# Retention attention and a gated feed-forward layer on one core: matmul groups and loads placed by the table that already places ScalarE's and VectorE's work

## The chip, the cores and the metric

One core of one Trainium2 chip. The metric is the device time of one execution in microseconds; the kernel before takes 275.86 us (median of 3 runs, 275.59 to 278.33).

## The reference

q, k and v are float32 of shape (8 batches, 8 heads, 576 positions, 64). The first half is attention without a softmax, with a decay per head; the second is a feed-forward layer of 512 to 2048 to 512 on the 4608 rows that the first half gives:

```python
scores = scale * np.matmul(q, k.transpose(0, 1, 3, 2))
gamma = 1.0 - 2.0 ** (-5.0 - np.arange(H))
Dmat = np.where(rel >= 0, gamma[:, None, None] ** rel[None], 0.0)   # rel = row - column
attn = np.matmul(scores * Dmat[None], v)
x = attn.transpose(0, 2, 1, 3).reshape(4608, 512)
h = x @ w_in
g = h * (1.0 / (1.0 + np.exp(-1.702 * h)))
out = g @ w_out
```

## The kernel before, in words

**Units and chunks.** The 4608 rows are 36 units of 128 rows; four units make a chunk of 512 rows, so there are nine chunks, 0 to 8. A unit is loaded in three parts: k and q (`load_kq`, line 358, q of units 1 and 2 by line 345) and v (`load_v`, line 371), all by DMAs that GpSimd issues. Unit 0's k and q come by SyncE (`load_kq0`, line 378).

**Attention of a unit.** k and q are transposed, by TensorE for units 0 to 7 (`transpose_pe`, lines 497 and 502, copied out by line 515 on ScalarE or 518 on VectorE) and by DMA for the others (`dma_transpose`, line 532, issued by SyncE). v is scaled by powers of the decay (`scale_v`). Then follow 64x64 matmuls: `scores` (line 638), masked out of PSUM by VectorE (`scores_out`, line 647); the state, k transposed times v (`state_half`, lines 544 and 554, in the first units; `state_both` and `state_sum` with a cast on ScalarE later); `values` (line 660) and `inter` (line 622), which make x; and `x_out` (line 675) or `x_out_pair` (line 685), which multiplies by a factor table `gq` and writes the transposed x, `xT`. The tables `vfac`, `gq` and `gpow` are made at the start with exponentials on ScalarE (lines 439, 447, 453); `gq_next` (line 470) makes the later parts of `gq` on VectorE from `gpow`.

**Feed-forward of a chunk.** In chunks 0 and 1 the product x times w_in is made directly (`up_group`, line 711, and `up`, line 697), and ScalarE applies the gate function straight from PSUM (lines 716 and 702). In chunks 2 to 8 seven products of half size replace eight (class `UpSet`, matmuls at line 954): four sets of 256 features, each with seven steps of four 128x256 matmuls and a pair of PSUM banks of its own, (X, Y), (C, D), (A, B) and (K, E). ScalarE copies some products out (line 965), VectorE adds others (line 969), ScalarE applies the gate function (line 978). The second matrix is used in the same way (class `Pair`, matmuls at line 821): VectorE makes sums of g (line 802), seven products of 16 matmuls follow, called first to seventh, ScalarE copies (line 834), VectorE adds (line 837), and the rows are stored (`store`, line 726).

**What sets the order.** The program is recorded as a list of operations (`Program.op`) with what each reads and writes; waits come out of that in `settle`. Each engine then executes its own list in the order of a key. For TensorE, GpSimd and SyncE the key is the place in the recording. For ScalarE and VectorE it is looked up in `PLACES` by stage ("early", "first", "second", "mid", "last"), which says how far ahead or behind an operation stands; the lead-in is recorded before any stage, and there these two engines too keep the order of the recording. Five chunks, 3 to 7, share the rows of "mid". `PADS` gives numbers of empty instructions (`nop`) that are put before matmuls in certain stretches.

**The lead-in** (`lead_in`). TensorE first runs matmuls on a cleared tile (`warm_quads`, line 1100, and `warm`, line 1093) whose results nobody reads, and some more between the first units. The recording puts all exponentials of ScalarE first and then one gate function on a dummy tile (`gelu_table`, line 1106), so that the load of that function's table stands ahead of the first real one. GpSimd issues the v of unit 0, units 1 and 2, the first two pairs of w_in (`load_win`, line 393: two DMAs a call, 256 columns), unit 3, four more calls of w_in, and so on.

Of the kernel before, what the change touches and what calls it, by code (L numbers as in the profile page):

```python
# [11 lines left out]
B, H, S, DH = 8, 8, 576, 64  # L12
# [18 lines left out]
class Program:  # L31
# [3 lines left out]
    def __init__(self, places, pads=()):  # L35
        self.ops = []
        self.pads, self.gaps, self.spare, self.wide = pads, 0, 0, True
        self.writers, self.readers = {}, {}
        self.places, self.kind, self.turn = places, None, 0
        self.met = {}  # L40
# [22 lines left out]
    def op(self, eng, fn, reads=(), writes=(), dma=None, ndma=1, after_ops=()):  # L63
# [14 lines left out]
        if eng in ("act", "dve"):  # L78
            o.key, o.label = self.place(eng)
# [73 lines left out]
    def emit(self, eng, handle, sems):  # L153
# [16 lines left out]
PLACES = {  # L170
    ("early", "act"): (
# [8 lines left out]
    ),  # L180
    ("early", "dve"): (
# [1204 lines left out]
```

## Time and profile before

| what | value |
|---|---|
| median of 3 runs | 275.86 us |
| the profiled execution's own time | 277.19 us |
| its span, first to last instruction | 275.4 us |
| TensorE busy | 267.3 us (97%), 4402 matmuls |
| VectorE, ScalarE, GpSimd busy | 215.4, 176.1, 136.4 us |
| mean granted TensorE clock | 0.994 |
| first matmul of the feed-forward layer (line 711) | starts at 14.28 us |
| first product with w_out (line 821) | starts at 54.51 us |
| last matmul ends, span ends | 272.66, 275.4 us |

The profiled execution took 277.19 us, 1.79 us more than its span. Lines of a profile name the source line, the engine, the operation and what it writes and reads; times are microseconds unless marked ns. In the timeline a bracket gives the idle time of the engine before an instruction and what ended it.

### The profile page before, as it was taken

How to read it: one execution, taken by the hardware profiler on the slowest of the kernel's cores; microseconds unless marked ns; L12 is line 12 of the kernel's file. 1: busy time of each engine (PE TensorE's matmuls, PEld its weight loads, DVE VectorE, ACT ScalarE, POOL GpSimd, SP SyncE). 2: the span in 40 equal slices, each digit the busy share in tenths (PEclk: the TensorE clock that was granted, in tenths of full speed). 3: DMA queues.
4: the chain of work that ended last, by engine and by line, in shares of the span. 5: the costliest groups of instructions: out<-in, count | busy, mean ns of one | idle time of the engine just before them, and what ended most of it. 6: DMA issues, size and time to landing. Idle time of an engine off the chain costs nothing.

```text
span 275.4 us, 10512 instructions
## 1 busy us (share of the span) xinstructions
PE 267.3 (97%) x4402; PEld 222.6 (81%) x4402; DVE 215.4 (78%) x420; ACT 176.1 (64%) x345; POOL 136.4 (50%) x167
## 2 busy tenths in 40 slices
PE   8789999999999999999999999999999999999996
PEld 6467568888888788878887888788878887888785
DVE  6825457959999889769996999688969996976681
ACT  7536775556937962796279627961796289608942
POOL 9999999400603927943970975096509020000000
PEclk9979999999999999999999999999999999999999
DMA  9999999999993967998998994999299435003004
GB/s 167 172 201 203 221 209 202 224 152 235 187 161 36 240 132 70 197 284 82 171 218 213 95 181 113 231 100 198 89 234 99 60 106 126 6 2 152 0 2 152
DMA packets 118029, 40.79 MB, mean 148 GB/s; under 512 B 104160, under 2 KB 111328, under 8 KB 117984
## 3 DMA queue, kind: packets, MB, share of 16 engines
q0 software_dynamic: 80800, 22.82, 72.2%
q1 hardware_dynamic: 36320, 16.00, 23.8%
q10 hardware_dynamic: 864, 1.31, 1.3%
q8 instruction: 36, 0.59, 0.9%
q14 instruction: 9, 0.07, 0.1%
HBM read 36.70 MB, written 9.44 MB: 168 GB/s over the span
## 4 chain that ended last, share of the span: by engine, by line
PE 85%; ACT 6%; POOL 3%; DMA 2%; DVE 2%; issue 1%; ACTq 0%; POOLq 0%
PE psB L821 20%; PE psA L821 16%; PE psX L954 4%; PE psK L954 4%; PE psA L954 4%; PE psC L954 4%; PE psD L954 3%; PE psY L954 3%; PE psE L954 3%; PE psB L954 3%; PE psB L711 3%; PE psA L711 3%; ACT vp L482 3%; DMA w_in_sb<-in_moe_w_in_dram 2%; PE psY L660 2%; PE psC L821 1%
## 5 line engine op out<-in xcount | busy, mean ns | idle before, releaser
L358 POOL DMA_DIRECT2D kqn<-in_k_dram x39 | 38.5, 1001 | 65.3 <-DMA kqT<-kqn 54.9
L978 ACT ACTIVATE gT<-part 128x512 bf16<-128x512 f32 (+1 forms) x56 | 46.7, 878 | 3.5 <-DVE part L969 3.5
L371 POOL DMA_DIRECT2D vn<-in_v_dram x40 | 40.0, 1018 | 0.1
L358 POOL DMA_DIRECT2D kqn<-in_q_dram x37 | 36.4, 1000 | 0.0
L486 POOL TENSOR_TENSOR vp<-vn,vfac 128x512 bf16<-128x512 f32 x22 | 23.0, 1086 | 21.9 <-PE psD L954 18.0
L965 ACT ACTIVATE part<-psX 128x512 f32<-128x512 f32 x14 | 8.4, 597 | 35.3 <-PE psX L954 35.3
L834 ACT ACTIVATE osb<-psB 128x512 f32<-128x512 f32 (+1 forms) x25 | 14.8, 591 | 23.9 <-PE psB L821 23.9
L821 PE MATMUL psB<-w_out_sb,gT 128*128 128x256 bf16 x224 | 27.0, 273 | 0.0
L821 PEld LDWEIGHTS psB<-w_out_sb,gT 128*128 128x128 bf16 x224 | 21.3, 98 | 4.2 <-DVE part L969 1.8
L591 ACT ACTIVATE kv<-stm 128x1024 bf16<-128x1024 f32 (+1 forms) x16 | 15.6, 976 | 4.8 <-DVE stm L582 4.7
L647 DVE TENSOR_TENSOR pm<-psC,mask 128x512 bf16<-128x512 f32 (+1 forms) x21 | 12.7, 606 | 6.2 <-PE psC L638 5.7
L821 PE MATMUL psB<-wsum,part 128*128 128x256 bf16 x136 | 16.3, 272 | 0.2
L821 PE MATMUL psA<-w_out_sb,gT 128*128 128x256 bf16 x136 | 16.3, 273 | 0.0
L821 PE MATMUL psA<-wsum,part 128*128 128x256 bf16 x136 | 16.3, 273 | 0.0
L685 DVE TENSOR_TENSOR xT<-psY,gq 128x512 bf16<-128x512 f32 x16 | 10.9, 683 | 6.1 <-PE psY L622 6.1
L802 DVE TENSOR_TENSOR part<-gT 128x1024 bf16<-128x1024 bf16 (+1 forms) x18 | 11.9, 667 | 4.3 <-ACT gT L978 2.0
L802 DVE TENSOR_TENSOR part<-part,gT 128x1024 bf16<-128x1024 bf16 (+1 forms) x18 | 12.0, 672 | 3.3 <-ACT gT L978 3.0
L821 PEld LDWEIGHTS psB<-wsum,part 128*128 128x128 bf16 x136 | 12.9, 97 | 2.0 <-DVE part L802 0.4
L821 PEld LDWEIGHTS psA<-wsum,part 128*128 128x128 bf16 x136 | 13.3, 98 | 1.5
L821 PEld LDWEIGHTS psA<-w_out_sb,gT 128*128 128x128 bf16 x136 | 13.2, 98 | 1.6
L821 PE MATMUL psA<-w_out_sb,part 128*128 128x256 bf16 x120 | 14.5, 273 | 0.0
L482 ACT ACTIVATE vp<-vn,vfac 128x64 bf16<-128x64 f32 x48 | 12.3, 337 | 2.2 <-DVE osb L837 2.2
(233 smaller groups left out, 778.1 us busy)
## 6 DMA issues: line engine op xcount, KB each, us to landing
vn<-in_v_dram POOLq DMA_DIRECT2D x32, 256.0 KB, 5.3
out_dram<-osb SPq DMA_DIRECT2D x26, 256.0 KB, 2.8
kqn<-in_k_dram POOLq DMA_DIRECT2D x31, 128.0 KB, 5.2
kqn<-in_q_dram POOLq DMA_DIRECT2D x31, 128.0 KB, 5.3
w_in_sb<-in_moe_w_in_dram POOLq DMA_DIRECT2D x16, 128.0 KB, 5.8
w_out_sb<-in_moe_w_out_dram POOLq DMA_DIRECT2D x4, 512.0 KB, 10.3
out_dram<-osb SPq DMA_DIRECT2D x10, 128.0 KB, 2.4
vn<-in_v_dram POOLq DMA_DIRECT2D x8, 128.0 KB, 4.9
```

The source lines that it names most:

```text
L358: e.dma_start(kqn[sl][p0 : p0 + n, which, :, :], src[b, :, s0 : s0 + n, :].rearrange("h p d -> p h d"),)
L371: e.dma_start(vn[sl][p0 : p0 + n, :, :], v[b, :, s0 : s0 + n, :].rearrange("h p d -> p h d"))
L482: op("act", lambda e, h=h: e.activation(vp[u % NVP][:, h, :], vn[sl][:, h, :], AF.Copy, scale=vfac[:, ty, h : h + 1]), reads=[f"vn{sl}"] + ...
L486: op(eng, lambda e: e.tensor_tensor(vp[u % NVP].ap(), vn[sl].ap(), vfac[:, ty, :, None].to_broadcast([P, H, DH]), ALU.mult), reads=[f"vn{s ...
L591: op("act", lambda e: e.activation(kv[:, i0 % NKV : i0 % NKV + n, :, :], stm[:, i0 % 8 : i0 % 8 + n, :, :], AF.Copy), reads=[f"stm{(i0 + i ...
L647: op("dve", lambda e: e.tensor_tensor(pm[(u0 // 2) % 2][hh][:, c0:c1].rearrange("p (a i) -> p a i", i=64), ps32(SB[hh])[:, c0:c1].rearrang ...
L711: op("pe", lambda e, a=a, f=f, i=i: e.matmul(bank[b][:, n * i : n * i + n], w_in_sb[:, a, P * f : P * f + P], xT[c % 2][:, a, P * lo : P * ...
L802: op("dve", lambda e, d=d, x=x, y=y, alu=alu: e.tensor_tensor(d, x, y, alu), reads=kx + ky, writes=kd)
L821: op("pe", lambda e, x=x, y=y, t=t, s=not more and t == 0 and k == 0, z=k == NF // 2 - 1: e.matmul(bank[b][:, 256 * t : 256 * t + 256], x, ...
L834: op("act", lambda e: e.activation(dst[0], src[0], AF.Copy), reads=src[1], writes=dst[1])
L954: op("pe", lambda e, x=x, y=y, i=i, s=not more and i == 0 and k == 0, z=k == 1: e.matmul(bank[b][:, 256 * i : 256 * i + 256], x, y, start= ...
L978: op("act", lambda e: e.activation(dst, src, AF.Gelu_apprx_sigmoid), reads=reads, writes=[g_key(self.c, f0 + 2 * i + q, j) for i in range( ...
```

## The change

TensorE's groups of matmuls, GpSimd's work, which is nearly all DMA issues, and SyncE's DMA issues get keys from `PLACES` too, and the lead-in becomes two stages of its own, "start" and "lead", so that everything is placed by the table. A group on TensorE is a run of matmuls recorded one after another from the same source line.

```diff
-    def place(self, eng):
-        if self.kind is None:
-            return len(self.ops) / 1e6, None
+    def place(self, eng, fn):
         n = self.met.get(eng, 0)
-        self.met[eng] = n + 1
+        if eng == "pe":
+            n, line, at = self.met.get(eng, (-1, None, None))
+            new = fn.__code__.co_firstlineno
+            n += at != len(self.ops) or (new != line and line not in self.fill)
+            self.met[eng] = n, new, len(self.ops) + 1
+        else:
+            self.met[eng] = n + 1
         row = self.places.get((self.kind, eng))
...
-        if eng in ("act", "dve"):
-            o.key, o.label = self.place(eng)
+        o.key, o.label = self.place(eng, fn)
```

All rows of `PLACES` are new, `PADS` falls from 483 empty instructions to 223, and the recording of the lead-in changes a little: three more filling matmuls (one of 512, one of 128, one of 256 columns), the state of unit 2 before its mask, two `up_group` calls later or earlier.

```diff
 PADS = (
-    0, 0, 0, 48, 0, 0, 63, 0, 0, 111, 0, 0, 75, 0, 0, 72, 0, 0, 114, 0, 0, 0, 0, 0, 0,
+    0, 0, 24, 0, 0, 0, 0, 0, 0, 0, 0, 0, 0, 4, 0, 87, 0, 0, 108, 0, 0, 0, 0, 0, 0,
 )
...
         def lead_in():
+            pr.stage("start")
+            op("dve", lambda e: e.memset(warmt.ap(), 0.0), writes=["warm"])
+            warm_quads(NQUAD)
+            warm(44, "A", 64)
+            pr.stage("lead")
...
-            warm(2)
+            warm(3)
             scores(2)
             scale_v(2)
+            state_half(2, 0)
+            warm(1, "B", 128)
             scores_out(2, 1, 0)
             scores_out(2, 1, 1)
             up_group(0, 0, 2, 0, 2, "A")
-            state_half(2, 0)
-            up_group(0, 2, 2, 0, 2, "B")
             gq_next(2)
             block1(2)
+            up_group(0, 2, 2, 0, 2, "B")
...
+            up_group(0, 0, 4, 2, 3, "A")
             transpose_pe(3, 1, "D")
             transpose_copy(3, 1, "D", "act")
-            up_group(0, 0, 4, 2, 3, "A")
             scale_v(3)
+            warm(2, "E", 256)
             scores(3)
...
-            warm(1, "E", 256)
```

What comes out of the new keys, read from the order of the two built programs (line numbers of the kernel before):

- **GpSimd, lead-in.** Before: v0, unit 1, unit 2, w_in columns 0 to 511 (two calls), unit 3, w_in. After: v0, k1, q1, k2, v1, v2, q2, v3, q3, k3, then w_in columns 256 to 511, columns 0 to 255, 512 to 767, k4, and so on.
- **TensorE, lead-in.** Before, from the scores of unit 2 on: up A (features 0, 1), state 2, up B (2, 3), attention of unit 2, transposes 3, up A (0 to 3 of unit 2's rows), scores 3, state 3, up B (4, 5), attention of unit 3, up A (4, 5), up B (6, 7), up C, up A, up B. After: scores 2, values 1, state 2 (first half), transposes 3, state 2 (second half), up B (2, 3), filling, scores 3, attention of unit 2, state 3, up A (0, 1), up B (4, 5), up A (0 to 3 of unit 2's rows), attention of unit 3, up B (6, 7), up A (4, 5), transposes 4, up B, up C, up A.
- **ScalarE, lead-in.** Before: 8 `vfac`, 4 `gq`, 4 `gpow`, table load, dummy gate function, then copies and gate functions alone; two table loads in all. After: table load, 8 `vfac`, copies, 4 `gq`, copies, `gpow` 1, copies, `gpow` 3, table load, gate function B (2, 3), table load, `gpow` 2, copy of the state of unit 3, table load, gate functions A (0, 1), B (4, 5), A (unit 2's rows), table load, `gpow` 4, table load, gate functions B (6, 7), A, and so on. Six table loads in all. A wait for a matmul stands at the gate function itself, behind the table load. `gelu_table` comes far behind.
- **VectorE, lead-in.** Setting up `iota_k` (line 429), which `vfac` waits for, moves behind the copies of unit 0's transposes.
- **Chunks 3 to 7, TensorE.** Before, the steps of sets X and C go in turn to their end, then those of A and K. After, the first steps of A and K stand between those of X and C, and the last steps of C and X between those of A and K; X's first step stands before the seventh product of the chunk before. The two blocks of attention keep their places, after the second and after the fifth product; inside them the state comes first or last.
- **GpSimd, chunks 3 to 7.** `scale_v` stands among the loads of the next chunk's units instead of behind them, so that the k of one unit and parts of two others are issued behind it. **SyncE**: two of the DMA transposes are issued between the stores of a chunk.

More of the change, by code (lines that the diff above doesn't have):

```diff
@@ L170 @@
 PLACES = {
-    ("early", "act"): (
[8 rows of a table removed]
+    ("start", "dve"): (
+        -9584670,
+    ),
+    ("start", "pe"): (
+        -8800216, -8582703,
+    ),
+    ("lead", "sp"): (
+        -451697, -452173,
+    ),
+    ("lead", "pool"): (
[4 rows of a table added]
+    ),
+    ("lead", "dve"): (
[5 rows of a table added]
+    ),
+    ("lead", "act"): (
[4 rows of a table added]
+    ),
[5 rows of a table added]
+    ),
[5 rows of a table added]
+    ),
+    ("early", "act"): (
[9 rows of a table added]
     ),
     ("early", "dve"): (
[5 rows of a table removed]
[6 rows of a table added]
+    ),
+    ("early", "pool"): (
+        110206, 109859, 107357, 112473, 50897, -39076, 112855, 125682, 42485, 109146, 113018, 81942, 145058,
+        142043, 144901, 137192, 198067, 176992,
+    ),
@@ L187 @@
+    ("early", "sp"): (
+        -514600, -475513, -380993, -322704, -153042, -115303, 69107, -74529,
     ),
     ("first", "dve"): (
[3 rows of a table removed]
[4 rows of a table added]
+    ),
+    ("first", "pe"): (
+        -1937, -911, -20270, -13780, 8996, 9042, -570, 1909, 3048, 2016, 5822, 12976, 42978, 13882, 23184,
+        15326, 15338, 15367, 31518,
     ),
     ("first", "act"): (
-        -116183, -73138, -75013, -72486, -55435, 31948, -42066,
+        -202134, -204784, -158822, -158667, -158598, 19905, -133306,
+    ),
+    ("first", "sp"): (
+        -174005, -88323, -11463, -15312,
+    ),
@@ L216 @@
+    ("mid", "sp"): (
+        12098, 6275, 26602, 28763, 95465, 77092, 30886, 116485,
+    ),
[5 rows of a table added]
     ),
     ("last", "act"): (
[3 rows of a table removed]
[3 rows of a table added]
     ),
     ("last", "dve"): (
[3 rows of a table removed]
[3 rows of a table added]
+    ),
+    ("last", "sp"): (
+        90402, 21097, 55314, 210415,
     ),
@@ L1095, in warm @@
                    reads=["warm"], writes=[b])
+                pr.fill.add(pr.ops[-1].fn.__code__.co_firstlineno)
         def warm_quads(n):
```

27 lines of the change are left out of this document (20 added, 7 removed), and 106 rows, old and new, of the table PLACES.

## The prediction

> **What bounds the kernel now.** I read the page's slices first, then the idle times in TensorE's timeline, then the chain that ended last, then the other engines' timelines where TensorE waits or runs slowly. The slices:
>
> ```profile
> PE   8789999999999999999999999999999999999996
> ...
> PEclk9979999999999999999999999999999999999999
> ```
>
> TensorE is busy from end to end, and only the third slice (14 to 21 us) has a lowered clock. Its timeline, its real work from 14 us on:
>
> ```profile
> 14.28 1.60 PE L711 MATMUL psA<-xT,w_in_sb 128*128 128x256 bf16 x8 [1.62 <-DMA w_in_sb<-in_moe_w_in_dram]
> ...
> 16.17 1.89 PE L711 MATMUL psB<-xT,w_in_sb 128*128 128x256 bf16 x8
> ...
> 19.57 1.07 PE L711 MATMUL psA<-xT,w_in_sb 128*128 128x128 bf16 x16 [0.31 <-DVE xT L675]
> ...
> 25.60 1.04 PE L711 MATMUL psB<-xT,w_in_sb 128*128 128x256 bf16 x8
> 26.48 1.03 PE L697 MATMUL psA<-xT,w_in_sb 128*128 128x512 bf16 x4
> ```
>
> The first product with w_in waits 1.62 us for its DMA, and the first two groups take about twice the 0.87 us that such a group takes later. The windows by half microseconds say why:
>
> ```profile
> 14.50:15.00 0.50, 0.50 (x5) 0.40 (x4) 0.00 (x0) 0.00 (x0) 0.50 (x2) 0.62 2.28 172
> ...
> 17.50:18.00 0.50, 0.50 (x6) 0.09 (x5) 0.00 (x0) 0.00 (x0) 0.50 (x2) 0.50 1.41 189
> 18.00:18.50 0.50, 0.50 (x37) 0.43 (x40) 0.00 (x0) 0.40 (x1) 0.50 (x2) 0.97 1.44 193
> ```
>
> (PEclk is the third number from the right: half from about 14.6 to 18.03.) After 30 us TensorE's bracketed idle times are 0.20, 0.42, 0.27 and 0.32 us, 1.2 in all. From there on the kernel is TensorE's own work: a chunk takes 27.4 us (150.57 to 177.97) whatever else happens. So lost time in the lead-in goes straight to the end, and time can be won only in small joints. The chain at such a joint, the end of an up phase:
>
> ```profile
> 175.19 0.44 PE psA L954 x4
> 175.63 0.46 PE psK L954 x4
> 176.09 0.49 PE psB L954 x4
> 176.57 0.49 PE psE L954 x4
> 177.06 0.44 PE psA L954 x4
> 177.50 0.47 PE psK L954 x4
> ```
>
> **The change, part by part.**
>
> *1. w_in behind unit 3.* The loads on GpSimd:
>
> ```profile
> 7.67 2.47 POOL L393 DMA_DIRECT2D w_in_sb<-in_moe_w_in_dram  x4
> 10.10 0.93 POOL L358 DMA_DIRECT2D kqn<-in_k_dram  x1
> 10.99 0.93 POOL L358 DMA_DIRECT2D kqn<-in_q_dram  x1
> 11.86 0.94 POOL L371 DMA_DIRECT2D vn<-in_v_dram  x1
> 12.74 4.99 POOL L393 DMA_DIRECT2D w_in_sb<-in_moe_w_in_dram  x8
> ```
>
> Unit 3's three issues take 12.74 - 10.10 = 2.64 us and now stand first. The chain has the second half of the first w_in call issued at 8.29 and landed after 5.94 us; so the first w_in (columns 256 to 511, which TensorE uses first) lands at 8.29 + 2.64 + 5.94 = 16.87, and the first up group starts at 16.9: **+2.6 us**. Landings of w_in ran from 4.3 to 6.4 us, so 15.2 to 17.3. An early landing helps little: v3 must land before VectorE can scale it (issued 7.67, v's median 6.4 us, so 14.1), and then VectorE still has this scaling (0.68), a mask (0.41), `gq_next` (0.68), a mask and two `x_out` (0.41 each) before x of unit 1 is complete, about 16.8. That VectorE sets up `iota_k` late, so that `vfac` and the first `scale_v` start 1.5 us later, is swallowed by the same wait.
>
> *2. Work done ahead.* The transposes of unit 3 (8, at 18.64 and 18.88, 0.45 together) and two state halves (0.15 each) move before the first up group, and the 0.31 us idle at 19.57 goes: -1.05.
>
> *3. The clock.* Before, 16 matmuls of 256 columns took 1.61 + 1.82 us between 14.28 and 18.06 instead of 1.75: 1.7 lost. Afterwards TensorE idles at least as long before the first up group, so I let the clock drop again and come back at the same time; only 16.9 to 18.05 then pays half: 0.6, so -1.1. If it needs another stretch of the same length (3.4 us, to 21.45) it is +0.6; if it never drops, -1.7.
>
> *4. ScalarE's tables.* The table load costs:
>
> ```profile
> 5.51 1.28 ACT L1106 ACT_TABLE_LOAD   x1
> 6.80 0.21 ACT L1106 ACTIVATE tblt<-warmt 128x4 bf16<-128x4 bf16 x1
> ```
>
> Before, this switch is hidden. Now exponentials for `gpow` 2 and 4 stand between gate functions: four more loads. First pair: up B ends at 18.35, gate function (0.60) to 19.0, load 20.28, `gpow` 20.4, copy of the state 20.75, load 22.05, gate function A 22.65. TensorE meanwhile has filling 0.2, scores 0.25, attention of unit 2 0.5, state 0.15, up A and up B 0.87 each and 0.3 of joints: at 21.5 it needs bank A again and waits **1.15**. Second pair: up A' to 23.55, its gate function to 24.2, loads and `gpow` 4 to 26.9, gate function B to 27.5; TensorE reaches bank B at 23.55 + 0.7 (attention 3) + 0.87 + 0.44 + 0.45 (transposes 4) + 0.25 = 26.3 and waits **1.2**. Up B, C, A add 2.3: the lead-in's groups end at 29.8, where before they ended at 26.48, or 26.93 with the transposes of unit 4, which now lie before. **Sum of the lead-in +2.9** (2.6 - 1.05 - 1.1 + 2.35 = 2.8, the rest is rounding). Behind it wait ScalarE's copies of unit 4; they are 0.6 us each against 0.87 per up group, so the backlog drains. Bounds: +0.5 if both pairs are covered, +4.1 with the late clock and the latest landing.
>
> The Trainium skill, "ScalarE: Activation LUTs" (What ACT_TABLE_LOAD costs), advises batching calls by table set and puts a switch at 2.66 us, 1.28 for the load and 1.38 for a drain. The row has the 1.28 exactly and no drain: the load starts where the last `gpow` ends (5.03 + 0.48) and the next function at its end.
>
> *5. Chunks 2 to 8.* The order spreads the last groups of the up phase: between two uses of bank A or E stand four or five groups of 0.44 us instead of three, so the 0.46 to 0.49 above should become 0.44. That is 0.17 us an up phase (165.58 to 177.97 is 12.39 against 28 times 0.4365), times 7: **-1.2**. The first product of the chunk takes 1.91 instead of 1.75 and waits for the same addition, three groups back as before: 0. So bounds are 0 and -2.3 (0.33 times 7) for the waits. The extra breaks between 64x64 groups and products in chunk 2 cost 0.1 to 0.15 each: 0.15, within the rounding.
>
> *6. The queues.* GpSimd now has `scale_v` ahead of some loads of the next chunk: the k of such a unit is issued about 3.5 us after the up phase starts, lands 5.2 us later and goes through a 3.0 us transpose by about 14; scores need it after 12.4 + 3.5 us. Two transposes now stand ahead of a store, 5.4 us for four; the row buffers are needed again 12 us later. Both covered by about 2 us or more: 0, and 0.5 us a chunk if the cover fails (+3.5 over seven).
>
> *7. Empty instructions.* Chunk 7's up phase has none, chunk 6's 114; both periods are 27.40 us. 0. The four idles after 30 us (1.2) belong to orders that all change; I count 0, from -1.2 to +1.
>
> The tail (last matmul at 272.66, end at 275.4) keeps its last product, copy and store: 0. **Sum: +2.9 - 1.2 = +1.7.** Against the profiled execution's own 277.19 us that is 278.9; that run was 1.33 above the median, so I forecast 277.6 against 275.86.
>
> **The rivals.**
>
> *A: TensorE never waits after 30 us* (not slower). Place: every joint of chunks 1 to 8; price: the 0.33 us at the end of each up phase and at the first product, seven times, and the four idles, 3.5 us; it decides once more than 2.9 is found. 275.86 + 2.9 - 3.5 = 275.3. For it: the greater distances. Against: the first product keeps its distance.
>
> *B: the reloads hide.* ScalarE waits 3.63 us for psA at 15.92 before, so a load can vanish there; if other work fills TensorE, lead-in +0.5: 275.86 + 0.5 - 1.2 = 275.2. Against it: after each gate function ScalarE has 3.3 us to do and TensorE reuses the bank after about the same.
>
> *C: the new queues starve the steady chunks*, 0.5 us each: 275.86 + 2.9 + 3.5 = 282.3. For it: GpSimd is full for whole 10 us windows there (10.00 at 180 to 190). Against: 2 us of cover.
>
> *D: each table switch also empties the engine*, a load's length again four times: 277.6 + 4 times 1.28 = 282.7. The row at 5.51 speaks against it. By the Trainium skill's page above it would be 4 times 1.38, so 283.1.
>
> *E: nearly all excess in the joints goes* (0.57 us a chunk, from products of 1.85 to 1.91 instead of 1.75 too, 4.0 over seven) and the reloads hide: 275.86 + 0.5 - 4.0 = 272.4. Against: half of it stands where attention meets products, and those places stay.
>
> **How the numbers follow.** Forecast 46%, A 14%, B 14%, C 14%, D 4%, E 8%. 1% is 2.76 us, about what a measurement can tell from no change: below 273.1 faster, above 278.6 slower. Faster: E and 2% of A and B, 0.10. Slower: C, D and the part above 278.6 of the forecast's own range (276.2 to 279.6, three tenths of its 46%), 0.32. Within: 0.58. The range goes from 273.3 to 281.2: it leaves out E's lower side, D and most of C.
>
> **What would show it.** Right: in the changed profile the first line 711 group starts near 16.9, six table loads stand on ScalarE, TensorE idles about 1 us before two line 711 groups at about 22 and 27 us, and the first product with w_out starts about 2.5 to 3 us later than 54.51; later chunks take 27.2. Wrong: the first product at 54.5 or earlier, chunks below 27.0, or waits on DMA in the chunks.

## The result, and the profile after

The changed kernel takes 286.37 us (median of 4 executions, 285.06 to 288.19) against 276.7 us of the kernel before in the same sitting: 1.0349 times as long, 95% interval 1.0266 to 1.0432. That is slower, by 9.7 us; the forecast was 277.6 us and its range ended at 281.2. (Ratios leave out executions that lie over 1.5% above the fastest of their kernel.)

The slices of the page, TensorE's busy tenths and its granted clock, of the changed kernel:

```profile
PE   7796999999899999999999899999998999999995
...
PEclk9897999999999999999999999999999999999999
```

TensorE is still busy from end to end, 267.8 us of a span of 283.2, so busy time hides where 7.8 us went. But the clock is now low in two slices, the second and the fourth, where it was low in one, the third. The span, cut at four places in TensorE's timeline, tells more (starts and ends of the profiled executions, us; `no_reload` and `five` are runs told below):

| stretch | before | changed | no_reload | five |
|---|---|---|---|---|
| to the first group of `up` (line 796 after) | 26.48 | 31.41 | 29.25 | 26.24 |
| from there to the first product with w_out | 27.87 | 27.32 | 26.81 | 26.99 |
| from there to chunk 3's first product with w_out | 68.84 | 69.82 | 68.69 | 69.03 |
| from there to the end of the last matmul | 149.45 | 151.40 | 151.26 | 148.75 |
| tail | 2.76 | 3.25 | 3.19 | 2.98 |
| span | 275.4 | 283.2 | 279.2 | 274.0 |

The two profiled executions took 277.19 and 285.06 us, the one above its kernel's median and the other below, so their difference is 7.9 and not 9.7. Of the 7.8 us between the spans the lead-in has 4.9, the stretch up to chunk 3's first product 1.0, the rest 2.0 and the tail 0.5; the second stretch is 0.55 shorter. (The transposes of unit 4, 0.45 us, have moved from the second stretch to the first. The third stretch does not end at chunk 2's first product, because 32 matmuls of scores and 32 of values stand ahead of that product in the changed order and behind it in the kernel before; cut here, the third and the fourth stretch hold the same matmuls in both kernels. The timeline starts the first product with w_out of the kernel before at 54.35; the chain, from which the prediction's 54.51 came, gives starts some 0.1 to 0.2 later.) The lead-in, TensorE's timeline:

```profile
17.16 1.05 PE L810 MATMUL psB<-xT,w_in_sb 128*128 128x256 bf16 x8
...
20.27 1.03 PE L810 MATMUL psB<-xT,w_in_sb 128*128 128x256 bf16 x8
23.95 1.05 PE L810 MATMUL psA<-xT,w_in_sb 128*128 128x128 bf16 x16 [2.65 <-DVE pm L746]
...
25.68 1.89 PE L810 MATMUL psB<-xT,w_in_sb 128*128 128x256 bf16 x8
...
29.20 1.03 PE L810 MATMUL psB<-xT,w_in_sb 128*128 128x256 bf16 x8
...
31.41 1.03 PE L796 MATMUL psB<-xT,w_in_sb 128*128 128x512 bf16 x4
```

One idle time of 2.65 us stands before the group at 23.95, and the group at 25.68 takes 1.89 us, about twice the 1.05 of the others. GpSimd issues the first w_in at 10.26 us, 2.59 later than before, behind unit 3 as told:

```profile
9.38 0.90 POOL L457 DMA_DIRECT2D kqn<-in_k_dram  x1
10.26 3.73 POOL L492 DMA_DIRECT2D w_in_sb<-in_moe_w_in_dram  x6
```

ScalarE at the time of the idle stretch:

```profile
18.23 1.28 ACT L815 ACT_TABLE_LOAD   x1
19.53 0.60 ACT L815 ACTIVATE winsum<-psB 128x512 bf16<-128x512 f32 x1
20.14 1.28 ACT L552 ACT_TABLE_LOAD   x1
21.44 0.20 ACT L552 ACTIVATE gpow<-lng 128x4 f32<-128x4 f32 x1
21.55 0.36 ACT L653 ACTIVATE kv<-psK 128x256 bf16<-128x256 f32 x1
21.92 1.28 ACT L815 ACT_TABLE_LOAD   x1
...
25.66 1.28 ACT L552 ACT_TABLE_LOAD   x1
26.95 0.20 ACT L552 ACTIVATE gpow<-lng 128x4 f32<-128x4 f32 x1
27.16 1.28 ACT L815 ACT_TABLE_LOAD   x1
28.46 0.60 ACT L815 ACTIVATE winsum<-psB 128x512 bf16<-128x512 f32 x1
```

The loads are there as forecast, 1.28 us each, and each starts within 0.02 us of the end of the function before it. The Trainium skill, "ScalarE: Activation LUTs" (What ACT_TABLE_LOAD costs), has 2.66 us for a switch with its drain; no drain shows here either. The bracket at 23.95 names VectorE's mask, but in the built order the group waits for two other things: `x_out` of unit 2, which ends at 22.81 + 0.41 = 23.22, and the gate function that empties bank A, which ends at 23.21 + 0.60 = 23.81. The group starts 0.14 us after the later one, so ScalarE ends the wait. (`x_out` is late by the same loads: `gpow` 2 at 21.44 releases `gq_next`, and that `x_out`.) And the first load, at 18.23, is not hidden either: it stands behind `gpow` 3 at 18.02, and bank B has been full since 17.16 + 1.05 = 18.21.

The windows of TensorE's clock around the slow group (the third number from the right is the granted clock):

```profile
25.00:26.00 1.00, 1.00 (x43) 0.81 (x43) 0.22 (x1) 0.94 (x2) 1.00 (x3) 0.63 1.82 186
26.00:27.00 1.00, 1.00 (x7) 0.69 (x6) 1.00 (x3) 0.99 (x2) 1.00 (x3) 0.50 1.62 274
27.00:28.00 1.00, 1.00 (x9) 0.88 (x8) 0.13 (x1) 0.99 (x2) 1.00 (x3) 0.50 1.46 212
28.00:29.00 1.00, 1.00 (x12) 0.88 (x10) 0.00 (x0) 0.99 (x3) 1.00 (x3) 0.66 1.94 176
```

0.63 over the first microsecond means half clock from 25.26 on, 0.66 over the last until 28.68: 3.4 us, behind the idle time that began at 21.3. An earlier stretch of the same length (11.6 to 15.0) falls on filling matmuls and attention.

Later the chain that ended last runs through the loads again and again, where before it stays on TensorE: DMA has 13% of the whole chain and TensorE 68%, before 2% and 85%. One such place, in chunk 4, from the chain:

```profile
146.77 0.99 POOL vp L585
147.76 5.47 DMA kqn<-in_k_dram
...
153.24 1.24 SPq L631
...
154.58 6.85 DMA kqT<-kqn
...
161.47 0.21 PE psC L737
```

GpSimd scales a v (0.99) ahead of issuing a k; k lands 5.47 us later, SyncE issues the transpose then, and that takes 6.85 us. TensorE's scores at 161.47 wait 0.88 us for it:

```profile
161.47 0.21 PE L737 MATMUL psC<-kqT 64*64 64x64 bf16 x1 [0.88 <-DMA kqT<-kqn]
```

The times between the starts of the chunks' products (chunks 3 to 7) are 28.01, 28.59, 27.31 and 28.18 us, where before they were 27.36 to 27.40.

And in chunk 1, ScalarE and TensorE:

```profile
75.88 0.60 ACT L933 ACTIVATE osb<-psA 128x512 f32<-128x512 f32 x1 [1.82 <-DMA out_dram<-osb]
```

```profile
70.38 0.22 PE L666 MATMUL psK<-vp,kqn 64*64 64x64 bf16 x2 [0.63 <-ACT vp L581]
77.95 0.22 PE L666 MATMUL psK<-vp,kqn 64*64 64x64 bf16 x2 [1.24 <-ACT vp L581]
```

ScalarE's copy of chunk 1's first product waits for a store of chunk 0's rows, the `vp` behind it come later, and TensorE's state group at 77.95 waits for them. The group at 70.38 waits for a `vp` too, but ahead of that copy: ScalarE has scaled one part of v after another since 66.41.

### The profile page after: what moved, and what is told of

Read it like the earlier page. It is cut to its first block, busy times and chain, and to the rows that moved or that the text cites. A ratio compares the mean times of both kernels' runs of the same rounds, so it can differ in the third digit from the quotient of the medians.

```text
span 283.2 us, 10245 instructions
## 1 busy us (share of the span) xinstructions
PE 267.8 (95%) x4405; PEld 228.2 (81%) x4405; DVE 216.6 (76%) x420; ACT 183.2 (65%) x349; POOL 136.3 (48%) x167
## 4 chain that ended last, share of the span: by engine, by line
PE 68%; DMA 13%; ACT 6%; POOL 5%; DVE 4%; issue 2%; SPq 1%; ACTq 0%; DVEq 0%
PE psB L920 15%; PE psA L920 12%; DMA kqT<-kqn 5%; DMA kqn<-in_k_dram 3%; PE psX L1053 3%; PE psC L1053 3%; PE psA L1053 3%; DMA kqn<-in_q_dram 3%; PE psY L1053 2%; PE psK L1053 2%; POOL kqn L457 2%; PE psD L1053 2%; PE psA L810 2%; PE psB L1053 2%; PE psE L1053 2%
## 5 line engine op out<-in xcount | busy, mean ns | idle before, releaser
L470 POOL DMA_DIRECT2D vn<-in_v_dram x40 | 38.1, 997 | 24.4 <-DMA kqT<-kqn 24.3
L457 POOL DMA_DIRECT2D kqn<-in_k_dram x39 | 36.6, 996 | 19.8 <-DMA kqT<-kqn 19.8
L457 POOL DMA_DIRECT2D kqn<-in_q_dram x37 | 34.4, 984 | 13.3 <-DMA kqT<-kqn 8.5
L920 PEld LDWEIGHTS psB<-w_out_sb,gT 128*128 128x128 bf16 x224 | 21.9, 98 | 2.5
L746 DVE TENSOR_TENSOR pm<-psD,mask 128x512 bf16<-128x512 f32 (+1 forms) x21 | 12.8, 608 | 3.5 <-PE psD L737 1.9
L933 ACT ACTIVATE osb<-psA 128x512 f32<-128x512 f32 (+1 forms) x11 | 6.3, 576 | 12.5 <-PE psA L920 10.7
L936 DVE TENSOR_TENSOR osb<-psA,osb 128x512 f32<-128x512 f32 (+1 forms) x17 | 11.1, 654 | 4.1 <-PE psA L920 4.1
L1068 DVE TENSOR_TENSOR part<-psY,part 128x512 f32<-128x512 f32 x14 | 9.7, 691 | 5.8 <-PE psY L1053 5.6
L901 DVE TENSOR_TENSOR part<-gT 128x1024 bf16<-128x1024 bf16 (+1 forms) x18 | 11.6, 648 | 2.8 <-ACT gT L1077 1.4
```

The source lines that it names most:

```text
L457: e.dma_start(kqn[sl][p0 : p0 + n, which, :, :], src[b, :, s0 : s0 + n, :].rearrange("h p d -> p h d"),)
L470: e.dma_start(vn[sl][p0 : p0 + n, :, :], v[b, :, s0 : s0 + n, :].rearrange("h p d -> p h d"))
L746: op("dve", lambda e: e.tensor_tensor(pm[(u0 // 2) % 2][hh][:, c0:c1].rearrange("p (a i) -> p a i", i=64), ps32(SB[hh])[:, c0:c1].rearrang ...
L901: op("dve", lambda e, d=d, x=x, y=y, alu=alu: e.tensor_tensor(d, x, y, alu), reads=kx + ky, writes=kd)
L920: op("pe", lambda e, x=x, y=y, t=t, s=not more and t == 0 and k == 0, z=k == NF // 2 - 1: e.matmul(bank[b][:, 256 * t : 256 * t + 256], x, ...
L933: op("act", lambda e: e.activation(dst[0], src[0], AF.Copy), reads=src[1], writes=dst[1])
```

## The experiments

All ratios are to the kernel before, measured in the same sitting. A small function at the end of the file moves named operations in an engine's list ahead of another, or gives an engine, from a stage on, the order of the kernel before. Operations are named by stage and number in the recording.

### First, one suspect and three halves

`no_reload`: the changed kernel without table loads between gate functions.

```diff
+MOVES = [
+    ('act', [('lead', 13), ('lead', 15)], ('lead', 14)),   # gpow 2, gpow 4 ahead of gpow 3
+    ('act', [('lead', 16)], ('lead', 28)),                 # gelu_table ahead of the first gate function
+]
```

> The changed kernel with one engine's lead-in altered: on ScalarE gpow 2 and 4 stand beside gpow 3, and the dummy gate function stands ahead of the first real gate function; all else as changed. Theory 1 (the four extra table loads are the largest single loss: 2.65 us idle before the third line 810 group, and, because TensorE idles there, a second stretch of half clock from 25.6 to 28.7 us that costs some 1.5 us): no load after 20 us, no half clock after 16 us, the first product with w_out about 4 us earlier than 58.9, and 286.4 - 4.1 = 282.3 us. Theory 2 (the late w_in and a late chain on VectorE set the lead-in, the loads lie beside them): the third group starts under 1 us earlier, time 285 to 286.4. If only the idle time goes and the clock drops all the same: 283.8.

Measured: 281.94 us, 1.018 (1.0138 to 1.0221). The time is near that of theory 1, but its condition on the clock is not met. The 2.65 us idle are gone, and the first product with w_out starts at 56.06. The half clock is not gone: it lies from 11.5 to 21.7 us here, 10.2 us long, and makes the first line 810 group 1.89 us long. So the gain of 4.7 us came with a worse clock in the profiled execution.

`lead_old`, `rest_old`, `q_old`: three cuts between the orders of the two kernels.

```diff
+USE_OLD = [('lead', e) for e in ("pe", "act", "dve", "pool", "sp")]   # lead_old
+USE_OLD = [('rest', e) for e in ("pe", "act", "dve", "pool", "sp")]   # rest_old
+USE_OLD = [('rest', 'pool'), ('rest', 'sp')]                          # q_old
```

> Lead-in recorded and ordered as in the kernel before on all five engines, everything from the first whole group of chunk 0 on as changed. Theory 1 (the lead-in costs 4.4 us by the first product with w_out, chunks 1 to 8 lose 3.5 more by themselves): 286.4 - 4.4 to 5 = 281.5 to 282. Theory 2 (the losses after chunk 0 are only the lead-in's lateness handed on): 275 to 277, as before. Theory 3 (the new orders from chunk 0 on are the main loss): 284 or more.

> The changed lead-in on all five engines, everything behind it in the orders and with the empty instructions of the kernel before. Theory 1: 276 + 4.4 = 280.4 (280 to 281.5). Theory 2 (all from the lead-in): 284 to 286. Theory 3 (the lead-in is made up for later): 276 to 278.

> The changed kernel, but behind the lead-in GpSimd and SyncE keep the order of the recording as in the kernel before (loads ahead of scale_v, stores where they were recorded); TensorE, ScalarE and VectorE as changed. Theory 1 (the new queue orders make k late, transposes late and TensorE wait at 132.8, 161.5 and so on, 0.5 to 0.8 us in some of the chunks): 2 to 3 us less, 283.5 to 284.5, and no idle time of TensorE put down to the transposes' DMA. Theory 2 (these waits stand beside others of the same length): 286 or more.

Measured: 290.87 us (1.0517, 1.0478 to 1.0556), 287.16 (1.0385, 1.0322 to 1.0448), 294.82 (1.0646, 1.0609 to 1.0682). `lead_old` and `q_old` are slower than either kernel, and `rest_old` is not told apart from the changed one. By number `lead_old` and `q_old` fall under a theory with an open end (284 or more, 286 or more), and `rest_old` lies just above its theory 2; but no theory had the reason. It shows on ScalarE, first in `q_old`, then in `lead_old`:

```profile
56.25 0.35 ACT L581 ACTIVATE vp<-vn,vfac 128x64 bf16<-128x64 f32 x1 [10.49 <-DMA vn<-in_v_dram]
```

```profile
51.45 0.35 ACT L581 ACTIVATE vp<-vn,vfac 128x64 bf16<-128x64 f32 x1 [9.07 <-DMA vn<-in_v_dram]
```

The changed order of ScalarE scales v of unit 11 between chunk 1's gate functions, and the changed order of GpSimd loads that v ahead of w_out. With GpSimd's old order the load comes after w_out, ScalarE stands for it with gate functions queued behind, and TensorE idles 10.26 and 8.85 us. In `rest_old` the waits are spread: 1.48 us at 24.95, 2.10 at 30.21 for a gate function, 1.77 at 81.12 for a copy. These runs price a mismatch and not a part of the change; they say only that the orders of the engines are made for each other. Apart from this wait, `q_old` has middle chunks of 27.83, 27.34, 27.21 and 27.33 us, which pointed to the queues.

### Then, from no_reload on, one part at a time

`dve_first`: VectorE sets up `iota_k` and the masks first.

```diff
+    ('dve', [('lead', 10), ('lead', 11), ('lead', 12)], ('lead', 15)),   # iota_k and masks ahead of the first cast
```

> The kernel of run no_reload (281.9 us, 1.018 of before), with iota_k and both masks set up on VectorE before its two casts, where it waits 2.4 us for the first q, and not between the first attention steps. Theory 1 (the set-up in the middle delays the first attention by 1.5 to 2.5 us, TensorE idles between 7 and 10 us, and that is why the clock is at half from 11.3 to 21.7 us in no_reload): TensorE busy from 8 to 10 us, no half clock before 15 us, the first line 810 group at full speed (1.0 instead of 1.9 us) and about 1.5 to 2 us less in all, 280 to 280.5, 1.012. Theory 2 (the clock drops because of the lead-in's 64x64 groups and waits in any case): half clock all the same, 281 to 282.

Measured: 280.42 us, 1.0099 (1.0055 to 1.0144). The profiled execution has full clock throughout and its lead-in ends at 25.83. But the mean clocks of its ten executions go from 0.979 to 1.000, so the edit does not keep the clock up by itself. Theory 1 has the time right; its mechanism is not shown.

`win_first`: w_in ahead of unit 3.

```diff
+    ('pool', [('lead', 11), ('lead', 10)], ('lead', 14)),   # two calls of load_win ahead of load_v(3)
```

> The kernel of run no_reload with the first two calls of w_in issued ahead of the three loads of unit 3, as in the kernel before. Theory 1 (w_in's place is what makes the first line 810 group late): the group starts 2.5 us earlier (15.7 instead of 18.2), and 1 to 2 us less in all. Theory 2 (in no_reload TensorE is held back by the half clock and by VectorE's late chain, so that w_in has landed by the time it is wanted): 281.5 to 282, the first group within 0.5 us of 18.2.

Measured: 283.36 us, 1.0183 (1.0107 to 1.0258), no different from `no_reload`. The first line 810 group starts at 18.20 us, as there. Theory 2: the place of w_in sets nothing in this lead-in. Its clock was at half as well before that group (11.8 to 15.2 us), so the run does not say what the place of w_in would cost at full clock.

`nr_q`: GpSimd's and SyncE's old orders from chunk 3 on, so that the early orders stay together.

```diff
+CUT, USE_OLD = 6, [('rest', 'pool'), ('rest', 'sp')]   # stage 6 is chunk 3
```

> The kernel of run no_reload with GpSimd's and SyncE's orders of the kernel before in chunks 3 to 8 only; the loads for chunks 0 to 3 stay as changed, so that the early orders fit together. Theory 1 (the new queue orders cost the middle chunks their excess: between the starts of their products with w_out lie 27.96, 28.56, 27.18 and 28.24 us in no_reload, against 27.4 before): all four at 27.2 to 27.4, and 2.5 to 3 us less, 279.0 to 279.5. Theory 2 (the excess comes from TensorE's own new order): the four stay, 281.5 to 282.

Measured: 279.15 us, 1.0035 (0.9999 to 1.0071). The four periods are 27.61, 27.34, 27.18 and 27.34 us, and the chain of chunk 4 has no DMA in it any more; the up phase ends and its products follow at once:

```profile
150.85 0.44 PE psE L1053 x4
151.29 0.44 PE psK L1053 x4
151.72 1.75 PE psB L920 x16
153.47 1.75 PE psA L920 x16
155.22 0.15 PE psK L666 x2
```

Theory 1 holds. 1.018 to 1.0035 is 4.0 us; by the periods it is 2.5 us (111.94 to 109.47 over four chunks). Other profiled executions bear it out: the four periods come to 111.9 to 113.0 us in `dve_first`, `one_pair`, `fill` and `fill2`, with the new queues, and to 109.8 and 109.4 in `three` and `five`, with the old ones.

`nr_pool` and `nr_sp`: the same with one of the two queues.

```diff
+CUT, USE_OLD = 6, [('rest', 'pool')]   # nr_pool
+CUT, USE_OLD = 6, [('rest', 'sp')]     # nr_sp
```

> The kernel of run no_reload (1.018) with GpSimd's order alone taken back from chunk 3 on, SyncE as changed. Theory 1 (late issues of k, behind scale_v, are the loss in the middle chunks): most of nr_q's gain, 1.004 to 1.008. Theory 2 (SyncE's order, two transposes ahead of a store, is the loss): 1.015 to 1.018.

> The kernel of run no_reload (1.018) with SyncE's order alone taken back from chunk 3 on, GpSimd as changed. Theory 1 (GpSimd): 1.015 to 1.018, and TensorE still waits for the transposes' DMA. Theory 2 (SyncE): 1.004 to 1.008, and the waits for the store and the copy behind it go.

Measured: 277.27 us, 0.9996 (0.9965 to 1.0027), and 281.16 us, 1.0122 (1.0068 to 1.0176). By the times GpSimd's order alone brings the whole gain. Its profiled execution, the slowest of the ten with 279.57 us, shows it in three of the four periods only (27.46, 30.61, 27.18 and 27.34): in chunk 4, the second, TensorE stands idle at about 155 us for a reason that the profile does not name, and the clock is at half from 156.6 to 160.0. SyncE's alone brings a part by the times; in its trace three of the four periods are down too (28.76, 27.35, 27.17, 27.34), which suggests that a late k hurts only together with a transpose that is queued late behind it. Its executions ran at mean clocks of 0.982 to 0.994 and those of `nr_pool` at 0.992 to 1.000, so how much of the difference between the two is the queue stays open.

`before_reload` and `before_reload2`: the kernel before with the late `gpow` 2 and 4 alone.

```diff
-            g_powers()
+            g_powers((1, 3))
...
-            up_group(0, 0, 2, 0, 2, "A")
+            up_group(0, 0, 2, 0, 2, "A"); g_powers((2,))
...
-            up_group(0, 0, 4, 2, 3, "A")
+            up_group(0, 0, 4, 2, 3, "A"); g_powers((4,))
```

> The kernel before with one thing of the change alone: ScalarE's gpow 2 right behind the first gate function and gpow 4 behind the third, so that four more table loads fall between gate functions. Theory 1 (each pair holds TensorE up by 1.0 to 1.3 us, as forecast): 278 to 279, 1.007 to 1.010. Theory 2 (the price is what the changed kernel shows, 2.65 us idle and a stretch of half clock behind it, 4.1 in all): 280 or more. Theory 3 (both pairs are covered): 276 to 277.

> The kernel of run before_reload again, for its profile alone. Theory 1 (in the kernel before, the first gate function is done early enough that gpow 2 and gq_next come just as TensorE needs them): idle times of TensorE of 0.3 to 1 us at about 20 and 24 us and no second stretch of half clock. Theory 2: an idle time of over 2 us, with half clock behind it.

Measured: 278.51 us, 1.0044 (1.0012 to 1.0076), and 278.40 in the execution that the profile shows. The price in the kernel before is 1.2 us (0.3 to 2.1). That is about half of what theory 1 has, 1.0 to 1.3 us for each of two pairs; its range of 278 to 279 us is met only because the kernel before took 276.9 us in this sitting. TensorE's waits in it:

```profile
17.12 0.21 PE L622 MATMUL psX<-kqT,kv 64*64 64x64 bf16 x1 [0.94 <-ACT kv L554]
...
24.11 1.05 PE L711 MATMUL psB<-xT,w_in_sb 128*128 128x256 bf16 x8 [0.65 <-ACT winsum L716]
```

The loads at 15.30 and 17.09 us hold up a copy of the state, the later ones a gate function. The waits are under 1 us, and its mean clock is 1.000. So the same four loads cost a quarter of the 4.7 us that the changed kernel gained without them.

### The three repairs together

`three`: the moves of `no_reload` and `dve_first`, and the queues of `nr_q`.

> The changed kernel with the three repairs together: no table loads between gate functions (no_reload, 1.018), VectorE's set-up first (dve_first, 0.8% less), GpSimd's and SyncE's orders of the kernel before from chunk 3 on (nr_q, 1.45% less). Theory 1 (the three losses are separate and add up, and together they are the whole of what was lost): 1.018 - 0.008 - 0.0145 = 0.9955, 275.5 against 276.7. Theory 2 (they overlap: a later start hides a part of the late loads, or the reverse): 1.000 to 1.005.

Measured: 277.08 us, 0.9999 (0.9968 to 1.0029). Theory 2: they overlap, and `three` is not told apart from `nr_q` or from the kernel before. The terms of the sum were both read against `no_reload`, whose executions had low mean clocks (0.970 to 0.992, against 0.982 to 1.000 in `three`), so each may hold a part of the same thing. That is argued and not shown.

`three_c1`: TensorE's order of chunk 1 from the recording.

```diff
-    ("first", "pe"): (
-        -1937, -911, -20270, -13780, 8996, 9042, -570, 1909, 3048, 2016, 5822, 12976, 42978, 13882, 23184,
-        15326, 15338, 15367, 31518,
-    ),
```

> The kernel of run three, with TensorE's groups of chunk 1's products and attention in the order of the recording, so that the attention of units 8 and 9 stands behind the first two products of chunk 1, as in the kernel before, and not ahead of chunk 0's last product. Theory 1 (TensorE's waits for ScalarE's vp and for the transposes in chunk 1, 0.84 and 1.19 us in nr_q, come from that place): these waits go, 1 to 2 us less than three. Theory 2 (the other engines' orders are fitted to TensorE's changed one): new waits of the same size, as three or more.

Measured: 287.87 us, 1.0365 (1.031 to 1.042), eleven more than `three`. Theory 2, and far over the size that it gave. TensorE's waits:

```profile
PE psA L920 <- ACT osb L933: 3.7, 1, 3.7
PE psB L920 <- DVE part L901: 3.1, 1, 3.1
```

`four`: only the scores of units 8 and 9 and the state of unit 9 one product later.

```diff
+    ('pe', [('first', 2), ('first', 3)], ('first', 0)),
```

> The kernel of run three (0.9999 of before), with the scores of units 8 and 9 and the state of unit 9 behind chunk 0's last product on TensorE, one product later. Theory 1 (in three TensorE waits 1.30 us at 65.5 for these units' transposes, and the product of 1.75 us covers that): the wait goes, 1.0 to 1.3 us less, 0.995 to 0.9965, faster than both kernels. Theory 2 (the wait only moves to VectorE's masks or ScalarE's vp): 0.999 to 1.001.

Measured: 277.83 us, 1.0017 (0.9985 to 1.005): no gain that can be seen, so theory 1 falls.

### Which pair of loads, and the clock

`one_pair`: only `gpow` 2 moves up, the second pair of loads stays.

```diff
+    ('act', [('lead', 13)], ('lead', 14)),
```

> The changed kernel with gpow 2 beside gpow 3, so that the first pair of table loads between gate functions is gone and the second pair, around gpow 4, stays. Theory 1 (the first pair has nearly the whole price, since gq_next, x_out and the third group wait for gpow 2, and the clock drops behind that): near no_reload, 1.018 to 1.022. Theory 2 (each pair costs the same, as forecast): halfway, 1.026.

Measured: 280.98 us, 1.0134 (1.0078 to 1.0191), at mean clocks of 0.992 to 1.000. Against 1.0349 this is 5.9 us. By the times the first pair of loads has the price: with the second pair left in, the kernel is not slower than `no_reload`. But the clock was better here than in either (0.982 to 0.988 in the changed kernel, 0.970 to 0.992 in `no_reload`), so the second pair is not shown to be free. In the trace it is not: TensorE waits 1.65 us before 26.37, 0.14 us after the gate function that stands behind the second pair ends (25.63 + 0.60).

`fill`: the loads stay, and TensorE is kept busy while it waits.

```diff
-            warm(2, "E", 256)
+            warm(2, "E", 256); warm(11, "E")   # the eleven moved ahead of the group at 23.95
```

> The changed kernel with eleven more filling matmuls of 512 columns (2.4 us at full clock) on TensorE ahead of the third line 810 group, in the 2.65 us that it stands idle there; nothing else altered, the loads stay. Theory 1 (the idle time lowers the clock from 25.6 to 28.7 us, and that is 1.5 us of the loads' price): full clock from 22 us on, the groups of the lead-in end 1.5 us earlier, 286.4 - 1.5 = 284.9, about 1.029. Theory 2 (the clock drops there for another reason, or what it costs is made up later): 1.035.

Measured: 288.28 us in the median of four, from 282.91 at a mean clock of 1.000 to 290.50 at 0.982; the ratio, 1.0282 (1.0194 to 1.037), rests on the two fastest, 282.91 and 286.76. The lower clock did not vanish from all executions. In the profiled one, at full clock:

```profile
23.06 1.05 PE L810 MATMUL psA<-xT,w_in_sb 128*128 128x128 bf16 x16 [0.28 <-DVE pm L746]
...
28.30 1.03 PE L810 MATMUL psB<-xT,w_in_sb 128*128 128x256 bf16 x8 [1.65 <-ACT winsum L815]
```

The slow group is gone, and the second pair of loads comes out instead: 1.65 us for the gate function, which in the changed kernel lay under the half clock. The lead-in ends only 0.7 us earlier (30.73). Two delays stood beside each other.

`fill2`: seven more filling matmuls between 7 and 12 us and six ahead of the transposes of unit 4.

```diff
-            warm(1, "A", 256)
+            warm(1, "A", 256); warm(4)
...
-            warm(1, "A", 256)
+            warm(1, "A", 256); warm(2)
...
-            warm(1)
+            warm(2)
...
-            warm(2, "E", 256)
+            warm(2, "E", 256); warm(17, "E")   # eleven and six of them moved to the two waits
```

> The changed kernel with 24 more filling matmuls of 512 columns on TensorE in the lead-in, each where it stands idle: seven between 7 and 12 us, eleven ahead of the third line 810 group, six ahead of the transposes of unit 4; nothing else altered, the four extra loads and the queues stay. Theory 1 (the changed lead-in's idle stretches make the clock fall, at about 2 us for each stretch of 3.4 us at half): a mean clock of 0.994 to 1.000 in nearly all executions, 282.5 to 283.5 us, 1.022 to 1.025. Theory 2 (the clock follows something else, the mass of 64x64 groups and transposes, or what it costs is covered): 0.982 to 0.988 as before, 1.03 to 1.035.

Measured: 284.77 us, 1.0232 (1.0185 to 1.028); mean clock 0.998 or 1.000 in five of six executions. By its ratio theory 1 holds: 1.0349 to 1.0232 is 3.2 us, with an interval of 0.6 to 5.9 when the two are combined. Its trace does not bear out as much: the execution profiled (285.26 us, full clock) ends its lead-in at 31.20, 0.2 us before the changed kernel's, since the fillers take time too. The slices:

```profile
PEclk9999999999999999999999999999999999999999
```

`five`: run `three` with v of unit 1 issued earlier and four fillers.

```diff
+    ('pool', [('lead', 6)], ('lead', 7)),   # load_v(1) ahead of load_kq(2, 0)
```

> The kernel of run three (0.9999) with v of unit 1 issued ahead of k of unit 2, as in the kernel before (in three VectorE waits 1.53 us for it), and four filling matmuls of 512 columns between 7 and 12 us. Theory 1 (what three still loses in some executions is the clock, and its lead-in waits for v of unit 1): clock 1.000 in nearly all, 0.5 to 1 us less than three, 0.996 to 0.998. Theory 2 (the rest of three's time is TensorE's own work as in the kernel before): 0.999 to 1.002.

Measured: 276.59 us, 0.997 (0.994 to 1.0001), mean clock 0.999 or 1.000 in ten of twelve executions. It is the fastest kernel here by a hair, and its interval still touches the kernel before. Its profiled execution has a span of 274.0 us.

## Why the prediction was wrong, step by step

The direction was right in its own sum (+1.7) and the size was not: 9.7 us. Three steps failed: step 4 left the first table load out of the path, step 6 put a short transpose into a stretch where it is long, and step 3 took a gain from the clock where there was a loss.

*Step 1, w_in behind unit 3 (+2.6).* The first group came at 17.16 us, forecast 16.9. The number agreed, and by the trace w_in was not what it waited for: TensorE has no idle time ahead of the group, x of unit 1 is complete at 16.40 + 0.41 = 16.81 (the step had about 16.8 for that chain), and the state placed ahead of the group starts at 16.91. With w_in first again (`win_first`) it came no earlier than in `no_reload`. What a late group delays was in part filled with work done ahead, *step 2* (-1.05). `five`, where w_in still stands behind unit 3 and the first group starts at 16.09, ends its lead-in 0.24 us before the kernel before does, with full clock. The profiled kernel before has a stretch of half clock there, on which step 3 puts 1.7 us, and lacks the transposes of unit 4 (0.45); without the one and with the other its lead-in would end at about 25.2, an estimate. So steps 1 and 2 together cost about 1.0 in that trace, where the forecast had 1.55.

*Step 3, the clock (-1.1).* This step has the wrong sign. It took the profiled execution of the kernel before, at a mean clock of 0.994, as what this kernel does. In the comparisons of these runs 84 of 89 executions of the kernel before had 0.999 or 1.000, so there was next to nothing to win; the changed kernel had 0.982 to 0.988 in all four. Worse, the step let the clock depend only on the wait at 12 to 16 us. TensorE's thin stretch between 7 and 10 us (VectorE's set-up, which step 1 called swallowed by the same wait) and the 2.65 us that step 4 itself forecast as a wait (1.15) were each followed by a stretch of half clock. The first of them need not come: the profiled execution of `fill`, with nothing added between 7 and 12 us, had full clock throughout. By `fill2` the clock is worth about 3 us of the 9.7, with a wide interval.

*Step 4, ScalarE's tables (two stalls, 1.15 and 1.2).* Mechanism and path right, size off. The loads, their number and their duration are as forecast, and no drain came (rival D falls). The stalls measured 2.65 and, at full clock, 1.65 (`fill`, `one_pair`): 4.3 instead of 2.35. The term that failed is the first gate function, put at 18.35 to 19.0. It ran from 19.53 to 20.13, since a load of 1.28 us stands ahead of it that is hidden in the kernel before; the step counted it among the six and left it out of the path. Gate function A then ended at 23.81 and not at 22.65, and TensorE, at its group by 21.3, waited that much longer. By the times `one_pair` puts 5.9 us on the first pair, clock included; `before_reload` shows that the same four loads cost 1.2 us where the first load was hidden, the groups came earlier and the clock held.

*Step 5, chunks 2 to 8 (-1.2).* Right. An up phase of the steady chunks takes 12.55 us from its first group to its last in the kernel before (165.42 to 177.97). In `five`, with the queues mended, it takes 14.14 (163.21 to 177.35), and one product of 1.75 now stands inside it: 12.39, or 0.16 less, where 0.17 was forecast. From chunk 3's first product to the last matmul, with five up phases, `five` takes 148.75 us and the kernel before 149.45: -0.7, where five times 0.17 are 0.85.

*Step 6, the queues (0, "covered by about 2 us").* The largest error behind the lead-in, and rival C by its mechanism: +2.5 us by the four periods, 4.0 by the times of `nr_q`. The step had k issued 3.5 us after the up phase starts, landed 5.2 later and transposed in 3.0, at about 14, against a need at 15.9. In chunk 4 the up phase starts at 142.59; k is issued 5.2 us after that (the scaling of v ahead of it waits for TensorE), lands 5.5 later, and issue and transpose take 8.2: done at 18.8, needed at 18.0. Waits on DMA in the chunks were named beforehand as a sign of being wrong. The term that failed is the transpose, 6.85 us in the middle of the chunk's other loads where an easy one of 3.0 was put in. GpSimd's part is shown by the times of `nr_pool`; the store behind two transposes is not told apart from it.

*Chunk 1* was not in the sum. Up to chunk 3's first product the table has +1.0 us, and the waits at 70.38 and 77.95, 1.9 together, lie there. It does not belong to TensorE's new order as such: `no_reload` has -0.15 in this stretch and `five` +0.2, while the profiled `nr_q`, with the same order, has +1.2 (53.92 to 123.95). `three_c1` and `four` changed that order and gained nothing, the first at a cost of eleven microseconds. That part of the cause stays open.

*Step 7* (empty instructions, 0): `five` has the changed numbers of them and is no slower. The tail, 0 in the forecast, has 0.5.

What a sum of the parts gives: two stalls 4.3, the queues 2.5 to 4, the stretch of chunk 1 1.0, the tail 0.5, steps 1 and 2 up to 1, step 5 -0.7 (from chunk 3 on), together 7.6 to 10.1 at full clock, of 9.7 measured; with about 3 for the clock on top it is too much. Some of these lie beside each other, as `fill` shows for the clock and the second stall. What the runs show as a whole is that the kernel without the loads, with VectorE's set-up first and with the old queues is level with the kernel before (`three`); how the 9.7 us divide between waits and clock is not settled. How cause and effect lie between the clock and the longer executions is open as well: an execution whose loads land late may have both more idle time and a lower clock.

## What to carry to other kernels

When instructions are put into a chain, write the chain out from its first one, with everything that was hidden until then: the same four table loads cost 1.2 us in one order and several in another, where a load that nobody had waited for stood at the head of the chain. Cover has to be worked out from loaded durations, those of the same stage with the same neighbours in flight, and a load behind an instruction that itself waits for TensorE is late by that wait. Orders of several engines that were made together can't be cut anywhere: two of the three halves here were slower than either kernel, while GpSimd's order could be exchanged from chunk 3 on. A part is priced by moving single operations, or by a cut at a place where the orders still fit.

## What was not expected of the hardware

The granted clock falls after less idleness than I had thought: with TensorE 26% busy in one microsecond and 86 to 94% in the next three (8 to 12 us of the changed kernel), half clock followed from 11.6 on. In lengths it keeps to a grid: 3.4 and 3.4 us in the changed kernel, 10.2 in `no_reload`. The Trainium skill, "TensorE: Matmul & The Clock Gate" (What's actually happening), has a window of 3.41 us that runs freely and lets the clock fall after an idle window. The lengths agree. That the window has to be idle does not: 21.85 to 25.26 us, the window before the second stretch, had 2.1 us of idleness and then full work. Nor does idle time as the profile counts it decide alone. In the changed kernel TensorE is idle for 0.85 us from 4.78 to 8.19 and the clock stays up; it is idle for 0.87 from 8.19 to 11.60 and the clock falls. In `no_reload` the clock stays at half from 11.5 to 21.7 while TensorE is 91 to 100% busy in every microsecond. What else counts is not shown here.

The same build differs from execution to execution in this: `dve_first` had mean clocks of 0.979 to 1.000 and `fill` 0.976 to 1.000. The times go with the clock only loosely: in `fill` 282.91 us at 1.000 and 286.76 at 0.993, but the fastest execution of `dve_first`, 277.50 us, had 0.992. One profiled execution tells neither how often a stretch of half clock occurs nor that it belongs to the kernel. With TensorE kept filled (`fill2`, `five`) the clock was 0.994 to 1.000 in all eighteen executions.
